# One new issue order, and a new deal of the PSUM banks, for a fused attention, mixture-of-experts and MLP kernel

## The chip, the cores and the metric

The kernel runs on one core of a Trainium2 chip. The metric is the device time of one execution in microseconds (us); the median of three executions of the kernel before is 450.44 us (449.55 to 452.05).

## The reference

Three blocks follow one another on float32 data. Each is written here with what matters for the work on the engines.

```python
# 1. block attention: 2 x 8 heads, 768 positions, head size 64
k_sum = max of k over blocks of 32;  v_sum = mean of v over blocks of 32     # 24 blocks
scores = [ q k^T / 8 where |i - j| < 16, else -1e9 ;  q k_sum^T / 8 + log 32 ]
a = softmax(scores);   x = a @ [v ; v_sum]                                    # [2, 768, 512]
# 2. mixture of 4 attention experts, the best 2 of them for each position
logits = x @ w_gate;  w = softmax over the top 2
out = sum over e of  w[e] * ( causal softmax(q_e k_e^T / 8) @ v_e ) @ wo[e]   # q_e = x @ wq[e], ...
# 3. mixer
u = out + (x^T U V)^T            # rank 32 along the positions
result = u + relu(u @ w_ch1) @ w_ch2                                          # 512 -> 2048 -> 512
```

## The kernel before

All of it is one program on one core, with five engines that each work through a queue of their own in order: TensorE (PE) does matrix products, VectorE (DVE), ScalarE (ACT) and GpSimd (POOL) the rest, and SyncE (SP) starts the DMAs.

**The work** is cut into some 830 parts. A part is a small function, mostly a generator that yields between its steps: one step puts the matmuls on PE, the next one the instruction that takes their result out of PSUM, and so on. The parts that the text speaks of:

- Preparation: `load_k`, `load_q`, `load_v` (DMAs), `fill_k` (L317 copies the mask columns), `ksum` and `vsum` (block maxima and means of the keys and values; L333 and L340 are matmuls on a tile 32 columns wide, L337 and L343 the copies behind them).
- Attention, 48 slots of two heads by 128 queries: `a_scores` (L385, four matmuls onto column tiles 64 wide; DVE minimum L388, ACT exponential L391), `a_trans` (L396, two transposes over the full width; ACT copy L398), `a_pv` (L408, four matmuls onto 64-wide tiles; DVE L415 to L417 after each second), `a_out` (L424, transposes over the full width; ACT L429, DVE L239).
- Experts: `v_proj` (L569, 12 matmuls, full width), `qk_proj` (L620, 12 matmuls, full width; ACT L625, DVE L239, and four POOL copies in `hi_pool`, L236), `s_row` (L651, full width; DVE L659, ACT L662), `s_norm` (DVE L669 and L670, POOL L675), `t_bank` (L684, transposes; ACT L692 or DVE L690), `pv` (L704, matmuls onto 64-wide tiles; ACT L711, DVE L713 or L708).
- Weights that are made while the experts run: `late_woT` and `wo_split` (DMA, ACT, then POOL L470 and L489), `w1_load` (DMA, L245) and `w1_split` (DVE L253, ACT L255, DVE L257, ACT L264, POOL L266). `w1_load` puts its data where `late_woT` had its own, so its DMA waits for L470.
- The mixer: `w1c` (L497), `mlp1` (L816; ACT L821, DVE L823), `mlp2` (L829), `resid` (L838), `store` (L849, L851, L853).

**The order** is a table. Each part has a number u, and `TIMES[u][i]` is the place of its step i among all 1891 steps. A heap hands the steps out by that place; what a step issues goes to the end of each engine's queue. So the table sets, engine by engine, what stands behind what; when an instruction runs depends on the semaphores that it waits for. The PSUM bank of a part's result comes from `BANKS[u]`:

```python
heapq.heappush(todo, (TIMES[u][0] if TIMES else t, u, 0, fn, args))               # in at()
return BANKS[part] if BANKS else i                                               # in bank_of()
t, u, i, fn, args = heapq.heappop(todo)                                          # the loop at the end
heapq.heappush(todo, (TIMES[u][i + 1] if TIMES else t + wait, u, i + 1, part, ()))
# a_scores: out rows 64u..64u+63 of the bank, 120 columns per head
pe.matmul(scb[64 * u:64 * u + 64, hh], QAT[..][hh][..], KWT[..][hh][:, 2 * t + u, :], start=True, stop=True)
# a_trans: full width
pe.transpose(tb[0:KCOL, 128 * u:128 * u + 128], ex[:, u, :], ident)
```

Of the kernel before, what the change touches and what calls it, by code (L numbers as in the profile page):

```python
# [35 lines left out]
def f(ap):  # L36
# [12 lines left out]
    (20,), (0,), (50,), (2, 3, 5), (26, 32, 40), (1,), (4,), (10,), (12, 17, 41), (13, 35), (23,), (15, 21), (18,),  # L49
    (162,), (25, 51), (8,), (29, 53), (11,), (6,), (354,), (57, 61, 66), (85, 91), (100,), (56, 59, 63), (88, 99),  # L50
    (115, 121), (154, 167, 174), (68, 75, 82), (94, 104), (127,), (65, 72, 76), (90, 108), (130, 137), (159, 207, 216),
    (77, 89, 96), (120, 129), (139,), (73, 78, 84), (116, 135), (147, 161), (183, 187, 196), (106, 114, 118),
    (152, 160), (166,), (97, 102, 111), (158, 164), (169, 177), (194, 198, 208), (103, 109, 138), (163, 172), (189,),
    (110, 117, 125), (150, 175), (191, 200), (222, 237, 255), (122, 128, 146), (184, 192), (210,), (126, 132, 153),
    (186, 195), (212, 230), (249, 260, 268), (176, 193, 211), (219, 224), (242,), (201, 213, 218), (228, 232),
    (243, 247), (258, 270, 323), (173, 188, 202), (221, 239), (282,), (197, 220, 229), (257, 264), (285, 291),
    (302, 312, 338), (214, 223, 241), (246, 250), (284,), (203, 236, 245), (261, 289), (293, 304), (313, 317, 326),
    (231, 238, 254), (287, 292), (306,), (251, 263, 273), (297, 301), (309, 311), (319, 344, 360), (244, 278, 283),
    (298, 305), (329,), (290, 300, 308), (315, 321), (335, 363), (373, 388, 393), (267, 272, 279), (303, 316), (357,),
    (271, 288, 294), (322, 339), (358, 371), (394, 412, 416), (310, 318, 324), (349, 366), (377,), (325, 332, 346),  # L60
    (367, 376), (380, 383), (395, 402, 406), (333, 343, 355), (372, 378), (413,), (342, 348, 362), (368, 385),
    (414, 420), (423, 434, 447), (345, 356, 369), (397, 405), (451,), (382, 387, 407), (426, 431), (453, 455),
    (501, 504, 508), (389, 404, 415), (436, 450), (473,), (361, 379, 390), (445, 464), (475, 479), (503, 507, 521),
    (411, 422, 460), (481, 483), (492,), (408, 425, 438), (478, 487), (493, 516), (524, 549, 580), (448, 452, 458),
    (484, 491), (498,), (364, 410, 435), (482, 494), (500, 510), (526, 534, 541), (465, 472, 476), (528, 537), (543,),
    (468, 489, 497), (512, 520), (544, 559), (584, 587, 596), (488, 515, 522), (527, 530), (575,), (533, 538, 542),
    (551, 562), (578, 588), (602, 606, 615), (495, 499, 509), (565, 568), (592,), (545, 550, 558), (566, 590),
    (597, 607), (621, 647, 653), (536, 564, 572), (579, 583), (598,), (548, 556, 560), (581, 595), (601, 611),
    (620, 625, 631), (540, 563, 570), (617, 623), (639,), (593, 603, 609), (614, 627), (640, 642), (656, 659, 681),
    (589, 600, 612), (616, 619), (672,), (586, 618, 629), (658, 665), (674, 678), (700, 704, 715),  # L70
    (9, 14, 16, 19, 22, 24, 27, 30, 31, 33, 37, 38, 44, 46, 49, 52, 54, 58, 62), (36, 45, 47, 48, 64, 87, 92, 98, 144),
    (28, 34, 43, 67, 74, 80, 83), (79, 86, 93, 107, 136, 148, 157), (7, 42), (55, 60, 69), (39, 70),
    (95, 105, 113, 119, 123, 131, 156), (134, 149, 165, 171, 209, 217, 226), (71, 143), (124, 133, 141), (81, 142),
    (151, 170, 179, 185, 190, 199, 206), (233, 259, 266, 276, 280, 286, 296), (112, 145), (101, 168, 181), (180, 205),
    (240, 248, 256, 262, 269, 277, 295), (275, 334, 340, 353, 359, 365, 375), (155, 182), (204, 215, 227), (234, 253),
    (281, 314, 320, 327, 331, 341, 347), (384, 391, 399, 401, 417, 463, 469), (225, 235), (252, 328, 336), (307, 352),
    (433, 437, 441, 444, 449, 457, 459), (400, 443, 454, 474, 505, 511, 514), (337, 351), (418, 421, 428), (370, 430),
    (461, 471, 480, 486, 490, 496, 502), (506, 519, 532, 535, 539, 546, 552), (398, 429), (392, 409, 470), (462, 485),
    (265, 381, 386), (274, 330, 374), (140, 178, 299), (350, 396, 403), (456, 466, 477), (427, 440, 442),
    (419, 424, 432), (439, 446, 467), (513, 518, 523), (517, 525, 529), (531, 547, 561, 567, 571, 573, 622, 626, 630),  # L80
    (553,), (569, 576, 585, 591, 594, 599, 604), (557, 574, 577, 582, 608, 610, 613), (554,), (555,), (624, 633, 637),
    (634, 638, 644), (650, 652, 675, 679), (684, 689), (695, 699), (688, 692), (723, 741, 745), (636, 661, 667),
    (654, 657, 671), (682, 685, 690, 694), (702, 707), (729, 734), (643, 669, 676), (641, 673, 680),
# [1020 lines left out]
```

## Time and profile before

| what | value |
|---|---|
| median of three executions | 450.44 us (449.55 to 452.05) |
| span of the profiled execution | 451.4 us |
| PE busy | 432.3 us, 96% of the span |
| DVE, ACT, POOL busy | 52%, 49%, 40% |
| chain that ended last | PE 94%, DMA 2%, the rest 1% or less each |

The profile gives the span of the profiled execution, from its first to its last instruction; it is 1.0 us above the median of the three timed ones. A busy share is the time in which an engine has an instruction under way; the matmuls are pipelined and overlap, so a busy PE may still lose time between two of them, and that shows only in the distance from one start to the next. The chain follows the work back from the last instruction, at each step to what released it.

### The profile page before, as it was taken

Reading aid. Unit: us, or ns where it says so; the run is one execution under the profiler, and the core shown is the slowest. Engines: PE = TensorE matmul, PEld = TensorE weight load, DVE = VectorE, ACT = ScalarE, POOL = GpSimd, SP = SyncE. Lnnn points to the kernel's source line nnn. Section 1 sums busy time; section 2 is a strip of 40 time slices with the busy share of each in tenths; the row PEclk is TensorE's granted clock in tenths of the full one; section 3 lists DMA queues with packets and bytes.
Section 4 is the critical chain, followed back from the end, with each engine's and each line's share of the span. In section 5 each row is a group of like instructions: output and inputs, shape, how many; then the busy total and the mean of one; then the engine's idle time right before and its main releaser. Section 6 shows DMA issues by size and latency. Waiting matters only on the chain.

```text
span 451.4 us, 8626 instructions
## 1 busy us (share of the span) xinstructions
PE 432.3 (96%) x3224; PEld 376.2 (83%) x3224; DVE 233.7 (52%) x633; ACT 219.1 (49%) x581; POOL 178.4 (40%) x252
## 2 busy tenths in 40 slices
PE   0799999999999999899999999999999999999996
PEld 0687889999889888678889899898888888888985
DVE  4488755767656778968877545343412111111112
ACT  4377865656667587887655544344321111111112
POOL 6784884337765698862235423322210000000000
PEclk9999999999999999999999999999999999999999
DMA  8897742000000032252336342222103000000003
GB/s 211 173 258 186 194 113 57 2 1 0 19 3 1 1 105 82 69 185 73 111 121 185 112 172 93 70 97 91 48 26 115 0 1 0 0 2 0 1 0 139
DMA packets 14473, 35.19 MB, mean 78 GB/s; under 512 B 1888, under 2 KB 3168, under 8 KB 14432
## 3 DMA queue, kind: packets, MB, share of 16 engines
q1 hardware_dynamic: 14432, 34.65, 25.5%
q8 instruction: 25, 0.41, 0.4%
q14 instruction: 16, 0.13, 0.1%
HBM read 31.50 MB, written 3.15 MB: 77 GB/s over the span
## 4 chain that ended last, share of the span: by engine, by line
PE 94%; DMA 2%; POOL 1%; DVE 1%; SPq 1%; issue 1%; ACT 0%; POOLq 0%
PE ps L829 29%; PE ps L816 15%; PE ps L620 8%; PE ps L385 5%; PE ps L704 5%; PE ps L497 5%; PE ps L651 4%; PE ps L684 4%; PE ps L569 4%; PE ps L838 4%; PE ps L408 3%; PE ps L396 3%; DMA vb<-in_vW_dram 2%; PE ps L333 2%; PE ps L424 1%; PE ps L340 1%
## 5 line engine op out<-in xcount | busy, mean ns | idle before, releaser
L823 DVE SCALAR_TENSOR_TENSOR a<-ps,a 128x384 fp32r<-128x384 f32 x64 | 35.0, 556 | 114.6 <-ACT a L821 114.6
L821 ACT ACTIVATE a<-ps 128x384 fp32r<-128x384 f32 x64 | 30.7, 491 | 114.1 <-PE ps L816 92.4
L816 PE MATMUL ps<-x,w1h 128*128 128x384 f32 x256 | 73.3, 338 | 0.0
L829 PE MATMUL ps<-m,a 128*128 128x512 f32 x216 | 52.6, 392 | 0.0
L816 PEld LDWEIGHTS ps<-x,w1h 128*128 128x128 f32 x256 | 47.1, 188 | 2.1 <-issue 0.4
L829 PEld LDWEIGHTS ps<-m,a 128*128 128x128 f32 x216 | 40.3, 188 | 7.8
L236 POOL TENSOR_SCALAR a<-a 64x384 fp32r<-64x384 f32 x64 | 33.7, 528 | 24.0 <-ACT a L625 18.4
L816 PE MATMUL ps<-x,w1l 128*128 128x384 f32 x128 | 43.2, 337 | 0.0
L620 PE MATMUL ps<-x,m 128*128 128x384 f32 x192 | 36.9, 342 | 0.0
L620 PEld LDWEIGHTS ps<-x,m 128*128 128x128 f32 x192 | 33.1, 188 | 0.5 <-DVE gmx L607 0.4
L675 POOL TENSOR_SCALAR ex<-ex,rs,gate 128x256 f32<-128x256 f32 (+5 forms) x36 | 25.9, 729 | 10.9 <-DVE rs L670 7.5
L651 PE MATMUL ps<-a 128*128 128x384 f32 (+4 forms) x128 | 27.9, 337 | 1.4 <-DVE nmx L659 1.4
L829 PE MATMUL ps<-vb,a 128*128 128x512 f32 x108 | 26.6, 392 | 0.0
L829 PE MATMUL ps<-v,a 128*128 128x512 f32 x108 | 26.1, 394 | 0.0
L257 DVE SCALAR_TENSOR_TENSOR x<-x 128x256 uint32<-128x256 uint32 (+3 forms) x38 | 24.7, 653 | 2.5 <-ACT x L255 2.4
L662 ACT ACTIVATE ex<-ex,nmx 128x256 f32<-128x256 f32 (+5 forms) x36 | 23.4, 652 | 4.8 <-DVE nmx L659 4.4
L816 PEld LDWEIGHTS ps<-x,w1l 128*128 128x128 f32 x128 | 24.0, 188 | 1.7
L388 DVE TENSOR_REDUCE nmx<-ps 128x2 f32<-128x240 f32 x48 | 19.1, 404 | 11.2 <-PE ps L385 10.2
L659 DVE CUSTOM_DVE_ANT_0 ex<-ps,cc 128x256 f32<-128x256 f32 (+5 forms) x36 | 21.1, 598 | 6.3 <-PE ps L651 4.1
L829 PEld LDWEIGHTS ps<-v,a 128*128 128x128 f32 x108 | 20.3, 188 | 4.4
L829 PEld LDWEIGHTS ps<-vb,a 128*128 128x128 f32 x108 | 20.0, 188 | 3.6
L651 PEld LDWEIGHTS ps<-a 128*128 128x128 f32 x128 | 19.9, 189 | 3.7 <-DVE nmx L659 2.2
(218 smaller groups left out, 923.3 us busy)
## 6 DMA issues: line engine op xcount, KB each, us to landing
x<-in_w_dram SPq DMA_DIRECT2D x16, 512.0 KB, 3.6
x<-in_w_dram SPq DMA_DIRECT2D x20, 256.0 KB, 2.9
vb<-in_vW_dram SPq DMA_DIRECT2D x5, 585.0 KB, 4.9
a<-in_kP_dram SPq DMA_DIRECT2D x7, 416.0 KB, 5.2
out_dram<-a SPq DMA_DIRECT2D x10, 256.0 KB, 2.1
x<-in_wm_dram SPq DMA_DIRECT2D x4, 386.0 KB, 5.3
tb<-in_w_dram SPq DMA_DIRECT2D x6, 256.0 KB, 3.0
a<-in_w_dram SPq DMA_DIRECT2D x6, 256.0 KB, 2.8
```

Source lines behind the costliest of these rows:

```text
L236: pool.tensor_scalar(dst, src, 1.0, 0.0, op0=ALU.mult, op1=ALU.add)
L257: dve.scalar_tensor_tensor(low, high, 3, low, op0=ALU.logical_shift_left, op1=ALU.bitwise_or)
L385: pe.matmul(scb[64 * u:64 * u + 64, hh], QAT[p % NK][hh][:, QT * (2 * t + u):QT * (2 * t + u) + QT], KWT[p % 2][hh][:, 2 * t + u, :], star ...
L497: pe.matmul(acc, wo[k][:, int(a == 2), 128 * c:128 * c + 128], w[k][:, int(a == 1)], start=j == 0, stop=j == 11)
L620: pe.matmul(acc, (WML if wl else WMH)[k][:, 128 * e:128 * e + 128], xt(b, k, xl)[:, c], start=n == 0, stop=n == 11)
L651: pe.matmul(flat[:, base + c0:base + c1], QS[u][:, 128 * i:128 * i + 128], kk[:, c0:c1], start=x == 0, stop=x == 1)
L662: act.activation(ex[:, 0:W], ex[:, 0:W], AF.Exp, bias=nmx, scale=-1.0, accum_out=sums)
L675: pool.tensor_scalar(ex, ex, rs[:, i % 2:i % 2 + 1], gate[b][:, i, e:e + 1], op0=ALU.mult, op1=ALU.mult)
L816: pe.matmul(acc, (W1L if wl else W1H)[ff // 2][:, c, 128 * (ff % 2):128 * (ff % 2) + 128], cp(b, c, xl)[:, o], start=n == 0, stop=n == 5)
L821: act.activation(h, acc, AF.Relu)
L823: dve.scalar_tensor_tensor(l, acc, 0.0, f(h), op0=ALU.max, op1=ALU.subtract)
L829: pe.matmul(out_bank(b, 3 * j + t), a[:, 128 * t:128 * t + 128], w, start=False, stop=ff == 15 and x == 2, skip_group_check=True)
```

## The change

The two tables get other numbers; no other line changes. The kernel after has the same 1891 steps and the same 4103 instructions, in another order on each queue, and another bank for many results. The new tables take three lines more, so that L385 of before is L388 after, and so on for all that follows.

```diff
 TIMES = [
-    (20,), (0,), (50,), (2, 3, 5), (26, 32, 40), (1,), (4,), (10,), (12, 17, 41), (13, 35), (23,), (15, 21), (18,),
...
 BANKS = [
...
-    3, -1, -1,
+    -1, 3, -1, 1, -1, -1,
 ]
```

What the tables do to the queues is seen in the instructions themselves. First PE in the attention, some 20 us into the program. A row is a line of the code, the operation, what is written and read, the shape of the output and how many follow one another. `pt`, `c`, `w1h`, `w1l`, `ex`, `tb` and `vb` are buffers in SBUF, `cc` holds constants, `ps` is PSUM. 64x120 is a step of `a_scores`, 64x65 one of `a_pv` (four matmuls a step), 120x128 `a_trans` and 128x128 `a_out`. Before:

```order
L424 MATMUL ps<-cc,pt_82 128x128 x2
L396 MATMUL ps<-cc,tb 120x128 x4
L408 MATMUL ps<-vb,pt_79 64x65 x4
L408 MATMUL ps<-vb,w1h_88 64x65 x4
L424 MATMUL ps<-cc,pt_82 128x128 x2
L385 MATMUL ps<-pt_80,w1h_88 64x120 x2
L385 MATMUL ps<-c_81,w1h_88 64x120 x2
```

After, at the same point of the work:

```order
L411 MATMUL ps<-vb,pt_79 64x65 x4
L388 MATMUL ps<-pt_80,w1h_88 64x120 x2
L388 MATMUL ps<-c_81,w1h_88 64x120 x2
L411 MATMUL ps<-vb,w1h_88 64x65 x8
L411 MATMUL ps<-vb,pt_79 64x65 x4
L388 MATMUL ps<-pt_80,w1h_88 64x120 x2
L388 MATMUL ps<-c_81,w1h_88 64x120 x2
L388 MATMUL ps<-w1h_85,ex 64x120 x2
L388 MATMUL ps<-w1l_86,ex 64x120 x2
L399 MATMUL ps<-cc,ast 120x128 x2
```

The 64-wide steps, two or three at a time between full-width ones before, now stand seven in a row here (and two more `a_scores` steps right ahead of these rows). Over the whole program PE goes from full width to 64 wide 33 times before and 17 times after, and from 64 wide to full width 36 times before and 18 after. The 43 runs of 64-wide steps (28 in the attention, 15 of `pv`) become 24 (17 and 7). The switches to and from the 32-wide tiles of `vsum` and `a_mat` are 31 in both.

Second, DVE at the start, ahead of the first scores. `a_90` holds the mask columns, `ks` the block maxima, `pt_80` and `c_81` the keys of the first head pair. Before:

```order
L317 COPY pt_80<-a_90 64x1200
L368 TENSOR_SCALAR c_81<-ks 64x2x24
L337 COPY vt<-ps 128x128
L343 COPY vs<-ps 24x128
L874 MEMSET w1l_87 32x24
L317 COPY c_81<-a_90 64x1200
L388 TENSOR_REDUCE nmx<-ps 128x2 x5
```

After:

```order
L320 COPY c_81<-a_90 64x1200
L357 TENSOR_REDUCE ks<-a_89 128x24
L371 TENSOR_SCALAR c_81<-ks 64x2x24
L340 COPY vt<-ps 128x128
L371 TENSOR_SCALAR pt_80<-ks 64x2x24
L371 TENSOR_SCALAR c_81<-ks 64x2x24
L320 COPY w1h_85<-a_90 64x1200
L391 TENSOR_REDUCE nmx<-ps 128x2 x2
```

The mask copy into `c_81` stood behind the two copies of `vsum` and stands ahead of them now. On PE, the second matmul of that `vsum` (L340 before, L343 after) moves from ahead of all scores to behind two steps of them.

Third, POOL in the experts' stretch, some 165 us into the program. `v` is the split weight of `late_woT`, `a` the queries and keys of an expert, `ex` and `vb` rows of probabilities, `x` staging. Before:

```order
L470 TENSOR_TENSOR v_2112<-x_2119,v_2112 128x256
L236 TENSOR_SCALAR Usb<-x_2119 128x192
L470 TENSOR_TENSOR v_2110<-x_2119,v_2110 128x256
L675 TENSOR_SCALAR vb<-vb,rs_2272,gate_74 128x768
L236 TENSOR_SCALAR a_1266<-a_1266 64x384 x2
L675 TENSOR_SCALAR vb<-vb,rs_2272,gate_74 128x640
L675 TENSOR_SCALAR ex<-ex,rs_2357,gate_74 128x256
L675 TENSOR_SCALAR vb<-vb,rs_2357,gate_74 128x128
L489 TENSOR_TENSOR wol<-x_2119,woh 128x512
L470 TENSOR_TENSOR v_2109<-x_2119,v_2109 128x256
L470 TENSOR_TENSOR v_2111<-x_2119,v_2111 128x256
```

After:

```order
L678 TENSOR_SCALAR ex<-ex,rs_2281,gate_74 128x384
L239 TENSOR_SCALAR a_1068<-a_1068 64x384
L473 TENSOR_TENSOR v_1397<-x_1404,v_1397 128x256
L239 TENSOR_SCALAR a_1068<-a_1068 64x384
L473 TENSOR_TENSOR v_1394<-x_1404,v_1394 128x256
L473 TENSOR_TENSOR v_1396<-x_1404,v_1396 128x256
L473 TENSOR_TENSOR v_1395<-x_1404,v_1395 128x256
L678 TENSOR_SCALAR vb<-vb,rs_2293,gate_74 128x768
L239 TENSOR_SCALAR a_1068<-a_1068 64x384 x3
L678 TENSOR_SCALAR vb<-vb,rs_2293,gate_74 128x640
```

The four subtractions of `late_woT` stood in two pairs, eight instructions apart. They now stand almost together, ahead of one probability row and of the last three `hi_pool` copies of an expert's queries and keys.

## Rows read from the trace of the kernel before

**Rows 1.** The page: busy us, share of the span and instructions of each engine.
```profile
PE 432.3 (96%) x3224; PEld 376.2 (83%) x3224; DVE 233.7 (52%) x633; ACT 219.1 (49%) x581; POOL 178.4 (40%) x252
```
**Rows 2.** Busy time by stretch: us; PE, PEld, DVE, ACT, POOL; clock; DMA share; GB/s.
```profile
180.00:200.00 20.00, 18.38 (x132) 13.85 (x131) 15.72 (x49) 16.17 (x45) 16.15 (x23) 1.00 0.43 145
220.00:440.00 220.00, 220.00 (x1114) 194.51 (x1113) 78.25 (x155) 68.09 (x153) 37.44 (x38) 1.00 0.18 60
```
**Rows 3.** Timeline of PE, attention: start, us, line, tile, contraction*output rows, moving shape, matmuls.
```profile
23.58 0.45 PE L408 MATMUL ps<-vb,w1h 120*64 120x65 f32 x8
23.82 0.43 PE L385 MATMUL ps<-w1h,pt 128*64 128x120 f32 x4
...
31.88 0.42 PE L385 MATMUL ps<-c,w1h 128*64 128x120 f32 x4
32.24 0.44 PE L424 MATMUL ps<-cc,pt 128*128 128x128 f32 x2
32.51 0.60 PE L396 MATMUL ps<-cc,tb 128*120 128x128 f32 x4
33.04 0.46 PE L408 MATMUL ps<-vb,pt 120*64 120x65 f32 x8
33.33 0.45 PE L408 MATMUL ps<-vb,w1h 120*64 120x65 f32 x8
33.71 0.44 PE L424 MATMUL ps<-cc,pt 128*128 128x128 f32 x2
```
**Rows 4.** Chain of waits: start, us, engine and line, matmuls.
```profile
24.04 1.23 PE ps L385 x24
...
30.27 0.22 PE ps L396 x2
...
34.15 1.38 PE ps L385 x24
...
102.69 2.11 PE ps L620 x12
...
105.47 2.31 PE ps L620 x12
```
**Rows 5.** Timeline of PE at the start, with the idle time ahead and its releaser.
```profile
12.80 1.51 PE L333 MATMUL ps<-vb,cc 96*32 96x128 f32 x24 [12.80 <-DMA vb<-in_vW_dram]
14.72 0.62 PE L340 MATMUL ps<-vt,cc 128*24 128x128 f32 x2 [0.40 <-DVE vt L337]
15.77 0.67 PE L385 MATMUL ps<-pt,ex 128*64 128x120 f32 x4 [0.43 <-issue]
16.61 0.67 PE L385 MATMUL ps<-c,ex 128*64 128x120 f32 x4 [0.17 <-issue]
...
17.43 0.65 PE L385 MATMUL ps<-c,ex 128*64 128x120 f32 x4
```
**Rows 6.** Timeline of DVE at the start.
```profile
15.73 0.78 DVE L317 COPY c<-a 64x1200 f32<-64x1200 f32 x1
```
**Rows 7.** Timeline of PE in the experts.
```profile
186.67 0.85 PE L651 MATMUL ps<-a 128*128 128x320 f32 x4 [1.37 <-DVE nmx L659]
```
**Rows 8.** Timeline of DVE in the experts.
```profile
172.62 1.49 DVE L253 TENSOR_SCALAR x<-x 128x256 uint32<-128x256 uint32 x1 [0.68 <-POOL ex L675]
...
187.39 0.29 DVE L253 TENSOR_SCALAR x<-x 128x256 uint32<-128x256 uint32 x1
...
195.53 0.30 DVE L253 TENSOR_SCALAR x<-x 128x256 uint32<-128x256 uint32 x1 [2.14 <-DMA x<-in_w_dram]
```
**Rows 9.** Timeline of POOL in the experts.
```profile
172.65 1.30 POOL L489 TENSOR_TENSOR wol<-x,woh 128x512 fp32r<-128x512 f32 x1
...
187.35 0.89 POOL L675 TENSOR_SCALAR ex<-ex,rs,gate 128x512 f32<-128x512 f32 x1 [0.42 <-DVE rs L670]
```
**Rows 10.** Groups by line on POOL: busy us, mean ns, idle time before.
```profile
L470 POOL TENSOR_TENSOR v<-x,v 128x256 fp32r<-128x256 f32 x4 | 3.0, 748 | 0.0
```
**Rows 11.** DMA issues on the page: count, KB each, us from issue to landing.
```profile
x<-in_w_dram SPq DMA_DIRECT2D x20, 256.0 KB, 2.9
```

266 rows, old and new, of tables (BANKS, TIMES) are left out of this document.

## The prediction

> **What bounds the kernel now.** I read the page first, for the share of each engine [rows 1]: PE has an instruction under way in 432.3 of 451.4 us, and no other engine passes 52%. Then the chain of waits, of which the table above gives the shares: PE 94%. Then the busy time by stretches, to see whether the rest is spread out [rows 2]. It is not. From 20 us to the end of the mixer PE is busy throughout (220.00 of 220.00 from 220 to 440); the one stretch of 20 us that is not full is 180 to 200, where 1.62 us are idle, and most of that is a single wait of 1.37 us for the DVE minimum L659 [rows 7]. The rest of the idle time lies at the start: PE waits 12.80 us for the first half of the values [rows 5], and after its last matmul the end has a copy and a DMA. So PE's own work sets the end, and a change that only reorders can pay in three ways: fewer microseconds for the same matmuls, an earlier start, or less waiting.
>
> A busy PE is still not one that loses nothing. Its matmuls overlap, so the next view is the timeline of PE, read by the distance from one start to the next [rows 3], with the chain beside it [rows 4].
>
> **The change part by part.**
>
> *Switches of the tile width.* A step of `a_scores` (8 matmuls of the trace) takes 0.41 us when its own kind stands around it: 24 in 1.23 us [rows 4]; half a step is 0.205. A step of `a_pv` takes 0.24 (23.58 to 23.82) [rows 3], two transposes 0.22 [rows 4]. Now the same steps where the width changes [rows 3]:
> - Leaving 64 wide for the full width: the last half step of scores takes 0.36 instead of 0.205 (31.88 to 32.24), the last `a_pv` step 0.38 instead of 0.24 (33.33 to 33.71). That is 0.14 to 0.155 more. The first transposes after it take 0.27 instead of 0.22 (32.24 to 32.51), 0.05 more. Together 0.20 a switch.
> - Leaving the full width for 64 wide: four transposes take 0.53 instead of 0.44 (32.51 to 33.04), 0.09 more, and the first `a_pv` step after them 0.29 instead of 0.24 (33.04 to 33.33), 0.05 more. Together 0.14.
>
> The chain gives the same by another road [rows 4]: the first 24 score matmuls after full-width work take 1.38 instead of 1.23, 0.15 more, and 12 matmuls of `qk_proj` behind 64-wide work take 2.31 instead of 2.11, 0.20 more. Going from one half of the array to the other costs nothing: both column tiles are used within the 0.41.
>
> The order has 36 switches from 64 wide to the full width before and 18 after, and 33 the other way before and 17 after: 18 x 0.20 = 3.6, and 16 x 0.14 = 2.2, so 5.8 us less. If every switch were the 0.15 that the chain shows for one direction, 34 of them are 5.1; if every one were 0.20, 6.8. All of it lies on the path, since PE is what everything waits for in the stretches where these steps stand. The 32-wide tiles have 31 switches in both, and I cost them at nothing.
>
> *The start.* The same bytes lie ahead of the first `vsum`, so I leave PE's first matmul at 12.80. Its 24 matmuls end at 14.31 [rows 5]. Before, the scores begin at 15.77, do half a step, and stand until 16.61, because the mask copy into `c` runs only from 15.73 to 16.51 [rows 5, 6]. After, that copy stands ahead of both copies of `vsum` on DVE, and is done while PE is still in `vsum`. The scores run at half speed here: a step takes 0.82 (16.61 to 17.43) [rows 5] instead of 0.41, the lower of the clock's two levels by the spacing. Before, they are thus as far as if they had begun at 16.61 - 0.41 = 16.20 and never stopped. If they begin at 14.31 after, that is 1.9 us earlier, but the second matmul of `vsum`, which filled the hole before, now stands among the scores and costs its 0.62 [rows 5]: a gain of 1.3 at best. At worst the scores still begin where they do now, because of the queries that are loaded behind the values, and lose the 0.62. Between +0.6 and -1.3 I take -0.5, a little on the good side of the middle, since what ended the hole at 16.61 is gone for sure.
>
> *Waits in the experts.* Before, PE loses 1.6 us between 180 and 200 [rows 2]. The new order changes what queues where. Four POOL subtractions L470 of 0.75 us each, 3.0 in all [rows 10], stood in two pairs and now stand nearly together, ahead of three `hi_pool` copies that the scores of the seventh expert wait for. Behind them comes SP: the first DMAs of `w1_load` write where L470 reads, so they start later, and a DMA of that kind lands 2.9 us after its issue [rows 11]. Behind the DMA comes DVE: two L253 that wait for it stand ahead of an L659, of a copy of transposes and of an addition L713 on DVE's queue. Such a block can be survived: at 195.53 DVE stood 2.14 us for the DMA of an L253 [rows 8], in a stretch in which PE lost 1.6 us in all, with 1.37 of it elsewhere [rows 2, 7]. The bounds: no wait at all is 1.6 us less than now; one DMA in full and two of the subtractions are 2.9 + 1.5 = 4.4 more. I take +0.5, near the one block that the trace shows, which cost almost nothing.
>
> *A rule that speaks against it.* An L253 took 0.29 us at 187.39 and 1.49 at 172.62 [rows 8]; the slow one ran beside POOL's L489, from 172.65 to 173.95, the quick one beside POOL's L675, from 187.35 on [rows 9]. So DVE stood still for a POOL instruction with two tensor inputs, and not for one with a single one; L470 is of the first kind. The Trainium skill (SBUF — State Buffer, "SBUF: two separate sides") says that DVE and GpSimd share a port pair as an exclusive lock, the loser blocking for the other's whole instruction. The slow L253 agrees with that; the quick one, beside L675, does not. By the page each of three L253 in this stretch would wait for a POOL instruction of some 0.9 us, 2.7 of DVE's time; if half of it reached PE the sum would be about 1.3 higher.
>
> *The rest.* The mixer's order changes too, but it has no 64-wide tile, and PE is full in it [rows 2]; I cost it at nothing, with PE's own backlog as the cover. The end has the same copy and DMA. The new banks add no instruction; where one makes a matmul wait for an earlier reader, that is in the bounds of the waits.
>
> *The sum.* -5.8 - 0.5 + 0.5 = -5.8. The profiled span of 451.4 becomes 445.6; it lies 1.0 above the median of the timed runs, so the time is 444.6 us, 1.3% less.
>
> **The rivals.**
> 1. *The saving stays and the waits eat most of it.* One block of DVE in full and two subtractions, 4.4 us more than now instead of 0.5: 444.6 + 3.9 = 448.5. For it: POOL, ACT and DVE are each busy for 15.7 to 16.2 of 20 us from 180 to 200 [rows 2], so a late one catches up slowly. Against it: PE lost 1.6 us there under the old order, with a block of 2.14 in it.
> 2. *Slower: the queue of DVE behind two late weight loads sets the pace.* Both L253 wait out their DMA one after the other, 5.8 us, behind all four subtractions, 3.0, and the second meets a POOL instruction, 1.2 more (1.49 less 0.29 [rows 8]): 10.0 instead of 0.5 gives 444.6 + 9.5 = 454.1. It decides once the waits pass some 8 us more than forecast. Against it: the two DMAs overlap, and the minimum behind them has some slack.
> 3. *The waits go as well.* The stall of 1.37 us behind L659 [rows 7] belongs to one meeting of instructions that the new order breaks up, and the start gains its full 1.3: 451.4 - 5.8 - 1.3 - 1.6 = 442.7, less 1.0 is 441.7.
> 4. *The switches are not what costs.* If the extra time at a switch were waiting for operands that happens to fall there, it would be lost elsewhere: 450 to 451. Against it: the same 0.14 to 0.20 appear with four kinds of steps, and the steps that have their own kind around them never show them.
>
> **How the numbers follow.** The forecast has 0.60, rival 1 0.17, rival 2 0.06, rival 3 0.13, rival 4 0.04. The forecast's own range is 442.5 to 447, from the bounds of the switches (-6.8 to -5.1) and of the start. I reach to rival 3 below and past rival 1 above: 441.0 to 449.5, which leaves out rivals 2 and 4 and some edge. A change of under 0.5% (2.25 us) can hardly be told from none here. Below 448.2 lie the forecast, rival 3 and a third of rival 1: 0.79. Within 0.5% lie the rest of rival 1 and rival 4: 0.15. Above 452.7 lies rival 2: 0.06.
>
> **What would show it.** Right: in the chain, pieces of L385 and L408 (three lines later in the new numbering) that are longer and fewer, with the normal 0.41 and 0.24 a step inside; PE's summed busy time near 426; the scores without a hole before 16.6 us. Wrong: a stretch between 140 and 200 us in which PE is not full by 3 us or more, with a wait for DVE's L659 or POOL's L236 as its end, or an L253 on DVE with an idle time of some 3 us for a DMA ahead of it; or PE busy still near 432 with 34 fewer switches, which would be rival 4.

## The result, and the profile after

The changed kernel takes 455.19 us (median of 4 runs, 455.06 to 457.26), the kernel before 450.9 in the same runs (449.55 to 452.05): a ratio of 1.0112, 95% interval 1.0081 to 1.0144. It is slower by 4.3 us where 5.8 less were forecast. The time is outside the range, and it lies near rival 2's 454.1, but not by rival 2's mechanism.

All line numbers of the changed kernel are three higher. The page after, the busy time of each engine and the chain's shares by engine:

```profile
PE 429.8 (95%) x3224; PEld 377.3 (83%) x3224; DVE 229.0 (51%) x633; ACT 217.4 (48%) x581; POOL 179.3 (40%) x252
...
PE 82%; DMA 5%; DVE 5%; POOL 2%; ACT 2%; issue 2%; SPq 1%; POOLq 0%; DVEq 0%
```

PE has 2.5 us less under way than before [rows 1], in a span that is 2.0 longer (453.4). The prediction's signs were a busy time near 426 if it is right and near 432 for rival 4; 429.8 is neither, since a part of the waits counts as busy. The chain tells more: PE's share fell from 94% to 82%, and the DMAs and DVE stand in it now. Where that is, the busy time by stretches shows (us; PE, PEld, DVE, ACT, POOL; clock; DMA share; GB/s):

```profile
40.00:60.00 20.00, 17.01 (x314) 14.18 (x312) 13.66 (x44) 14.15 (x44) 13.49 (x15) 1.00 0.90 228
...
160.00:180.00 20.00, 18.95 (x136) 16.04 (x137) 13.38 (x43) 14.76 (x41) 16.90 (x26) 1.00 0.28 90
180.00:200.00 20.00, 18.38 (x145) 14.81 (x144) 17.00 (x50) 16.90 (x46) 15.34 (x20) 1.00 0.38 135
200.00:220.00 20.00, 18.68 (x137) 14.43 (x136) 14.24 (x33) 15.20 (x35) 6.86 (x7) 1.00 0.19 65
220.00:440.00 220.00, 220.00 (x1113) 194.44 (x1113) 74.67 (x154) 67.09 (x153) 36.09 (x37) 1.00 0.18 58
```

Four stretches of 20 us have holes where one had [rows 2]: 3.0 us in the attention, 1.0, 1.6 and 1.3 in the experts. The MLP is as it was. Holes understate waits, because a matmul is drawn as busy to its modelled end. So I also took, for every step of PE after 20 us, the distance from its first matmul to the next step's, less the usual distance of such a step in the trace of before, switches of the width included. What is left over, the waits by distance, sums to 1.2 us before (2.9 from 160 to 220 us, and -1.8 in small pieces elsewhere) and to 10.4 after (3.7 from 40 to 60 us, 6.7 from 160 to 220).

**The switches.** The rows that answer to [rows 3]; PE's timeline after, in the attention:

```profile
30.96 0.42 PE L388 MATMUL ps<-pt,w1h 128*64 128x120 f32 x4
31.17 0.42 PE L388 MATMUL ps<-c,w1h 128*64 128x120 f32 x4
31.52 0.65 PE L399 MATMUL ps<-cc,tb 128*120 128x128 f32 x4
32.05 0.44 PE L427 MATMUL ps<-cc,pt 128*128 128x128 f32 x2
32.42 0.43 PE L388 MATMUL ps<-pt,w1h 128*64 128x120 f32 x4
32.68 0.38 PE L388 MATMUL ps<-c,w1h 128*64 128x120 f32 x4
```

A half step of scores takes 0.21 (30.96 to 31.17) and 0.35 ahead of a switch (31.17 to 31.52); the first one behind a switch 0.26. Where the earlier trace had 0.36 and 0.205 [rows 3, 4], this one has 0.35 and 0.21: a switch costs what it did, and there are 34 fewer.

**The start.** PE's timeline after:

```profile
10.84 1.51 PE L336 MATMUL ps<-vb,cc 96*32 96x128 f32 x24 [10.84 <-DMA cc<-in_vB_dram]
13.80 0.67 PE L388 MATMUL ps<-pt,ex 128*64 128x120 f32 x4 [1.46 <-DVE pt L371]
...
15.75 0.62 PE L343 MATMUL ps<-vt,cc 128*24 128x128 f32 x2
...
19.16 0.61 PE L388 MATMUL ps<-c,ex 128*64 128x120 f32 x4
19.70 0.53 PE L399 MATMUL ps<-cc,tb 128*120 128x128 f32 x2
```

The hole of [rows 5] inside the scores is gone, as forecast, but a hole of 1.46 us ahead of them is new, for the DVE step L371 that fills the last columns of the scaled keys. The same 74 matmuls (24 of `vsum`, 2 of its second half, 48 of scores) end at 19.70 - 10.84 = 8.86 us behind the first one. Before they took 8.03, from 12.80 to the second of the next two rows, which are of the trace before:

```profile
20.51 0.39 PE L385 MATMUL ps<-c,ex 128*64 128x120 f32 x4
20.83 0.43 PE L333 MATMUL ps<-vb,cc 96*32 96x128 f32 x8
```

The two are not quite alike. Half steps stand 0.40 us apart at the start and 0.205 later; that halving came at 20.4 us before, 7.6 behind the first matmul, and at 20.0 after, 9.1 behind it. The second trace of before (before_again, below), where it also came 9.1 behind, took 8.41 for the same matmuls. Against that one the new start is 0.5 us longer and not 0.8.

**The attention.** The three longest waits of PE there:

```profile
43.35 0.87 PE L336 MATMUL ps<-vb,cc 96*32 96x128 f32 x24 [0.63 <-DMA vb<-in_vW_dram]
...
48.59 0.43 PE L388 MATMUL ps<-c,pt 128*64 128x120 f32 x4 [1.93 <-DMA pt<-in_qT_dram]
...
53.61 0.43 PE L388 MATMUL ps<-w1l,w1h 128*64 128x120 f32 x4 [0.37 <-DMA w1h<-in_qT_dram]
```

All three are loads. The longest load in the chain after, and the stretch of 40 to 60 us before:

```profile
43.37 10.10 DMA w1h<-in_qT_dram
```

```profile
40.00:60.00 20.00, 20.00 (x338) 16.09 (x338) 14.83 (x48) 16.21 (x53) 16.40 (x18) 1.00 0.69 194
```

SP's queue shows why they are late; its timeline before, and then after (issue, us, line, what is loaded):

```profile
29.07 0.33 SPq L325 DMA_DIRECT2D vb<-in_vW_dram  x1
29.44 2.36 SPq L303 DMA_DIRECT2D pt<-in_qT_dram  x2
```

```profile
34.74 0.33 SPq L301 DMA_DIRECT2D a<-in_kP_dram  x1
35.12 0.47 SPq L306 DMA_DIRECT2D pt<-in_qT_dram  x1
35.68 0.53 SPq L328 DMA_DIRECT2D vb<-in_vW_dram  x1
36.31 0.47 SPq L306 DMA_DIRECT2D w1h<-in_qT_dram  x1
36.83 2.10 SPq L518 DMA_DIRECT2D x<-in_wm_dram  x2
38.98 0.47 SPq L306 DMA_DIRECT2D pt<-in_qT_dram  x1
```

Before, both query loads of `load_q(4)` left from 29.44 on, ahead of the next key load. After, the key load `load_k(5)` stands first and waits at the head of SP's queue until 34.74 for its buffer, which POOL (L377) and DVE (L357) still read. The queries leave at 35.12 and, behind two loads of expert weights, at 38.98. In 40 to 60 us the DMA engines are 0.90 busy (0.69 before), and the chain has a query load of 192 KB issued at 43.37 that takes 10.10 us to land, where such loads took 5.2 to 5.5 in the median before.

**The experts.** PE, then DVE after (what answers to [rows 7, 8]):

```profile
172.78 1.04 PE L654 MATMUL ps<-a 128*128 128x384 f32 x5 [0.58 <-POOL a L239]
...
186.41 0.66 PE L687 MATMUL ps<-cc,ex 128*128 128x128 f32 x4 [1.62 <-POOL ex L678]
...
202.26 0.55 PE L687 MATMUL ps<-cc,ex 128*128 128x128 f32 x3 [0.87 <-POOL ex L678]
```

```profile
166.76 0.42 DVE L716 TENSOR_TENSOR c<-ps,tb 64x256 f32<-64x256 f32 x1 [2.57 <-ACT tb L714]
...
192.28 0.30 DVE L256 TENSOR_SCALAR x<-x 128x256 uint32<-128x256 uint32 x1 [1.87 <-DMA x<-in_w_dram]
```

The row on POOL and the row on ACT that stand behind two of these waits:

```profile
185.44 0.92 POOL L678 TENSOR_SCALAR ex<-ex,rs,gate 128x640 f32<-128x640 f32 x1
```

```profile
165.75 0.71 ACT L471 CAST v<-x 128x256 fp32r<-128x256 f32 x2 [2.48 <-PE ps L707]
```

The stall of [rows 7] behind the minimum is gone. POOL ends the waits now. The first, of 0.58, is the meeting that the prediction had in view: the `hi_pool` copies L239 run behind the four subtractions. The longest, of 1.62, is another: the normalisation L678 that feeds the transposes runs at 185.44, behind five copies and subtractions of other steps. The DVE wait of 2.57 comes from ACT, where a copy of weights L471 stood 2.48 us for the matmuls L707 that still read what it overwrites. One L256 waited 1.87 us for its DMA, like the one of 2.14 before [rows 8].

### The profile page after: what moved, and what is told of

It is laid out like the page before. It is cut to its first block, busy times and chain, and to the rows that moved or that the text cites. A ratio compares the mean times of both kernels' runs of the same rounds, so it can differ in the third digit from the quotient of the medians.

```text
span 453.4 us, 8600 instructions
## 1 busy us (share of the span) xinstructions
PE 429.8 (95%) x3224; PEld 377.3 (83%) x3224; DVE 229.0 (51%) x633; ACT 217.4 (48%) x581; POOL 179.3 (40%) x252
## 4 chain that ended last, share of the span: by engine, by line
PE 82%; DMA 5%; DVE 5%; POOL 2%; ACT 2%; issue 2%; SPq 1%; POOLq 0%; DVEq 0%
PE ps L832 29%; PE ps L819 15%; PE ps L623 6%; PE ps L388 5%; PE ps L500 4%; PE ps L841 4%; PE ps L572 4%; PE ps L654 3%; PE ps L707 3%; PE ps L411 2%; PE ps L399 2%; DMA w1h<-in_qT_dram 2%; PE ps L687 2%; DMA x<-in_w_dram 2%; DMA cc<-in_vB_dram 1%
## 5 line engine op out<-in xcount | busy, mean ns | idle before, releaser
L819 PE MATMUL ps<-x,w1h 128*128 128x384 f32 x256 | 74.5, 338 | 0.0
L239 POOL TENSOR_SCALAR a<-a 64x384 fp32r<-64x384 f32 x64 | 34.3, 535 | 21.3 <-ACT a L628 14.3
L678 POOL TENSOR_SCALAR ex<-ex,rs,gate 128x256 f32<-128x256 f32 (+5 forms) x36 | 26.2, 735 | 9.7 <-DVE rs L673 6.0
L662 DVE CUSTOM_DVE_ANT_0 ex<-ps,cc 128x512 f32<-128x512 f32 (+5 forms) x36 | 20.9, 595 | 4.5 <-PE ps L654 2.8
L256 DVE TENSOR_SCALAR x<-x 128x256 uint32<-128x256 uint32 (+3 forms) x38 | 16.1, 435 | 13.1 <-DMA x<-in_w_dram 11.5
```

The costliest lines, as they stand in the source:

```text
L239: pool.tensor_scalar(dst, src, 1.0, 0.0, op0=ALU.mult, op1=ALU.add)
L662: dve.tensor_tensor_reduce(out=ex[:, 0:W], in0=flat[:, base:base + W], in1=cmask[:, S - W:S], scale=-1.0 / 8.0, scalar=3.0e38, op0=ALU.add ...
L678: pool.tensor_scalar(ex, ex, rs[:, i % 2:i % 2 + 1], gate[b][:, i, e:e + 1], op0=ALU.mult, op1=ALU.mult)
L819: pe.matmul(acc, (W1L if wl else W1H)[ff // 2][:, c, 128 * (ff % 2):128 * (ff % 2) + 128], cp(b, c, xl)[:, o], start=n == 0, stop=n == 5)
```

## The experiments

Each run's ratio is to the kernel before on the same chip. "Waits" are the sums by distance described above.

**The attention's loads: e1_queries.** The changed kernel with three query loads moved:

```diff
 L328 DMA vb<-in_vW_dram
+L306 DMA pt_79<-in_qT_dram x2
 L301 DMA a_89<-in_kP_dram
-L306 DMA pt_79<-in_qT_dram
 ...
-L306 DMA pt_79<-in_qT_dram
```

> The order after, with three query loads moved forward on SP: both of the fifth head pair ahead of the sixth pair's keys, and the second of the sixth pair ahead of three weight loads of 386 KB; nothing else moves. In the trace of after PE loses 3.7 us more than its steps take between 40 and 60 us, 2.2 of it for one query load that landed 9.5 us after its issue, 0.6 for another, 1.0 for a load of values. Theory A (the place in SP's queue is the cause): the two query waits go, 2.8 us or more, about 452.3 against 455.2. Rival B (the DMA engines are simply full in this stretch, so that another transfer comes late in their place): within 1 us of 455.2.

Measured: 452.63 us (10 runs), ratio 1.0047 [1.0019, 1.0074], 2.6 below the change, as theory A had it. The waits from 40 to 60 us fell from 3.7 to 2.0; the two for queries are gone, and a transpose L399 now waits 0.88 us for its exponential. The late queries are a cause, worth 2.6 us.

**The weights of the experts: e2_weights, e3_both, e4_w2only.** The steps that load and split weights are put back among PE's steps where they stood before; all of them, all and the queries, and the queries with `w2_load` and `w2_split` alone. The first, on SP:

```diff
-L468 DMA x_1404<-in_woT_dram
-L488 DMA x_1404<-in_wo_dram x2
-L468 DMA x_1404<-in_woT_dram x3
+L488 DMA x_1404<-in_wo_dram
+L468 DMA x_1404<-in_woT_dram x2
+L488 DMA x_1404<-in_wo_dram
+L468 DMA x_1404<-in_woT_dram x2
```

> The order after, in which only the steps that load and split weights (late_woT, wo_split, w1_load, w1_split, w2_load, w2_split) stand where the order before had them against PE's work; in the order after they stand up to 136 steps earlier. Between 160 and 220 us PE loses 6.7 us in waits after, 2.9 before. Theory A (weights pulled forward overfill DVE, ACT and POOL while the experts need them): the 3.8 us go, 451.4 against 455.2. Rival C (the new order of the experts' own steps makes the waits): no change beyond 1 us, 454.2 to 456.2.

> Both edits together: the three query loads forward and the weight steps back. Theory A: the gains add, 2.8 + 3.8 = 6.6, about 448.6, below the kernel before. Rivals B and C: 454 to 456. If the saving of the tile switches (5.8) were not real, the waits gone would bring it to before's 450.9 and not below.

> The queries forward as in the first run, and of the weights only the second MLP matrix's loads and splits (w2_load, w2_split) back at their old place; late_woT and the splits of the first matrix stay pulled forward. If the w2 splits, which fill DVE to 9.84 of 10 us between 180 and 190, carry the loss in the experts: within 1 us of the run with both edits, about 449. If the early late_woT and w1 steps carry it (POOL's four subtractions together, DVE behind two late loads): about 452.

Measured: 459.25 (ratio 1.0192 [1.0138, 1.0246]), 456.93 (1.0136 [1.0092, 1.0179]) and 452.36 (1.0036 [1.0016, 1.0056]). None of the theories for the first two held: weights at their old places make it worse by 4 us. The matmuls L500 that use them stand earlier in the new order and then wait for the split (1.1 us for L267 alone). Behind that hole both traces also show the granted clock at its lower level, 0.50, from 190.8 to 194.2 us in e2_weights (PE was busy for 0.94 of the 2 us from 188 to 190); at half rate that is up to 1.7 us of the 4, by estimate. So the early weights are not shown to be a cause of the loss. `w2` makes no difference (0.3 us).

**The kernel before once more: before_again.** No edit.

> The kernel before once more, for a second trace of it. Its executions spread from 449.1 to 453.1 us; the trace that the prediction was read from has a span of 451.4, and a time is 1.8 above its span in all runs, so it was one of the longest. Theory: its length came from the start, where PE waited until 12.80 us for the values; here the first matmul starts near 11 and the span is 448 to 449.5, with the same waits later. Rival: the start is the same and the spread is in the experts' stretch (180 to 200 us).

One run of 452.85 us, span 451.0, first matmul at 12.74. The theory missed both numbers for this run (first matmul near 11, span 448 to 449.5), because the first load landed late again. With the profiles of the two price tests below (whose attention and experts are unchanged) it explains the span; see the last point of the next section.

**The same saving by other moves: e5_merged and e8_small.** The kernel before, with its own banks, and neighbours exchanged so that narrow steps stand together: in e5_merged 100 switches become 66, with steps up to 39 places away (its expectation says 28); in e8_small 78, none by more than 7 places. From e8_small, steps on PE:

```diff
 a_trans(13)
+vsum(3).0
 a_scores(18)
-vsum(3).0
 ...
 a_scores(20)
+a_scores(19)
 a_trans(16)
 a_out(11)
-a_scores(19)
 a_trans(15)
```

> The order and banks before, with 21 local moves of one to four PE steps past a neighbouring run of steps, so that PE changes tile width 66 times instead of 100, as often as in the order after; no step stands more than 28 of 1891 places from its old one, and the DMAs stay where they are. By the distances of starts in the trace of before, the switches that go are worth 5.8 us. Theory (a switch costs 0.14 to 0.20 us and the loss after is waits alone): 450.6 - 5 = 445.5, 444.5 to 447. Rival 4 of the prediction (the time at a switch is a wait that would fall elsewhere): 450 to 451.

> The kernel before with its own BANKS, and only those neighbours in its order exchanged that save a switch of the tile width at a distance of at most 7 places (14 exchanges: switches 100 -> 78, where the change and the earlier merged order go to 66; 92 of the 1891 steps stand elsewhere, none by more than 7 places). Theory A (each switch costs its 0.14 to 0.20 us everywhere, and what ate the saving so far were the long displacements, by which a step comes before its data or a load behind another load's wait): TensorE's work falls by 22 x 0.17 = 3.7 us, waits grow by under 1.5 us, time 448 to 449 (ratio about 0.994). Rival B (whatever groups the narrow steps makes waits as large as the switches it saves, however short the distance, since the narrow steps are the ones that hand work to the other engines and their results are then wanted closer together): work falls by the same 3.7 but waits grow by 3.5 or more, time 450.5 or more (ratio 0.999 or above).

Measured: 461.2 (ratio 1.0204 [1.0163, 1.0245]) and 454.75 (1.0092 [1.0071, 1.0114]). Both have fewer switches, and both lose more to waits by distance: 12 us more than before in e5_merged, 6.4 in e8_small. The trace of e5_merged is of its quickest execution, 457.89 us at a mean granted clock of 0.999; the other five, 459.60 to 462.44, show 0.991 to 0.996, so part of the median is the clock. PE's timeline of e8_small:

```profile
36.10 0.87 PE L335 MATMUL ps<-vb,cc 96*32 96x128 f32 x24 [0.37 <-ACT ex L393]
...
39.75 0.43 PE L398 MATMUL ps<-cc,ex 128*120 128x128 f32 x2 [0.30 <-ACT w1h L400]
...
43.25 0.46 PE L410 MATMUL ps<-w1l,pt 120*64 120x65 f32 x8 [0.43 <-DVE vs L345]
```

Before, no such wait stood between 20 and 60 us. The first two are at the very places of the diff: `vsum(3)` pulled ahead of a score step meets a bank that an exponential still reads, and a transpose pulled closer to its forerunner meets ACT's copy. They are short, and by distance there are nine of over 0.25 us from 35 to 80 us. In e5_merged neither theory nor rival came near 461.2. In e8_small rival B held in time: moves of a few places undo the saving. But both runs keep banks that were dealt for the old order, and the first of these waits is for a bank. No run here has these orders with a new deal of the banks, nor the change's order with the banks of before, so the two parts of the change, order and banks, are not told apart.

**Moves in the experts: e6_moves.** e1_queries with nine steps moved between 160 and 190 us; for one, the weight copies behind the copies of `pv` on ACT:

```diff
 L665 ACTIVATE vb,sums
+L714 COPY tb<-ps x2
 L471 CAST v<-x
 L471 CAST v<-x
-L714 COPY tb<-ps x2
```

> The order after with the query loads forward (the first run), and in the experts three things moved: POOL's second normalisation of the seventh expert's last rows directly behind the first instead of six POOL instructions later; late_woT's four ACT copies behind the ACT copies of pv, which they held up by 2.5 us while PE still read the values they overwrite; two of its four POOL subtractions and the two DVE steps that wait for the next weights behind the work of the scores. In the trace of the first run PE loses 6.0 us from 160 to 220, of it 1.45 at the first of these, 0.86 + 0.49 + 0.32 + 0.21 at the others. Theory A' (queue places of single instructions make the waits): 2 to 3 us less than 452.6, about 450. Rival (DVE and POOL are simply overfull there, and a wait removed comes back at the next step): 452 or more.

Measured: 453.76, ratio 1.0068 [1.0041, 1.0096]. The waits aimed at shrank (1.45 to 0.3 us), and a new one of 2.6 us by distance came at a scores step in the same stretch:

```profile
174.45 0.90 PE L654 MATMUL ps<-a 128*128 128x320 f32 x2 [1.99 <-ACT pt L695]
```

Here too the granted clock falls: it is 0.50 from 174.5 to 177.9 us, after PE was busy for 0.46 of the 2 us from 172 to 174. The time is the rival's (452 or more), and the ratio lies within the interval of e1_queries.

**The price of a switch by itself: p1_apart to p4_f32_together.** The MLP, where PE never waits. Two of the six matmuls of each of 64 tiles become 64 columns wide, apart (two round trips of the width) or together (one); in the first pair in the MLP's own type, in the second in float32 as the narrow matmuls of the attention are:

```diff
-pe.matmul(acc, (W1L if wl else W1H)[...], cp(b, c, xl)[:, o], ...)
+p = slice(0, 64 if n in (1, 3) else 128)       # together: (2, 3)
+g = f if n in (1, 3) else lambda ap: ap        # second pair only
+pe.matmul(acc[p], g((W1L if wl else W1H)[...][:, p]), g(cp(b, c, xl)[:, o]), ...)
```

> The kernel before, with the second and the fourth of the six matmuls of each MLP tile (64 tiles, line 816, in 220 to 440 us, where TensorE never waits) made 64 columns of the tile wide instead of 128, a wide one between them: no instruction more, two round trips of the tile width per tile. It leaves out the other half of these two products. Theory A (a change of width to 64 and back costs 0.20 + 0.14 us, as read from the distances of steps): 128 round trips x 0.34 = 43.5 us more, time about 494. Rival B (the switches are not what the time goes into; the distances at switches are long for another reason, the narrow matmuls' own first and last columns or the cold load of weights): the narrow matmuls take as long as wide ones and the time stays within 2 us, 449 to 453.

> As the run before it, but the third and the fourth of the six matmuls are the narrow ones, side by side: the same instructions, one round trip of the width per tile. It leaves out the other half of these two products. Theory A: 64 x 0.34 = 21.8 us more than before, about 472.5, and 21.8 less than with the two apart. Rival B (a narrow matmul itself costs more, whatever stands beside it): the same time as with the two apart, both above before. Rival C (no price at all): within 2 us of before.

> As the run with the narrow matmuls apart (second and fourth of the six of each MLP tile 64 columns wide), but these two also in plain float32, as every narrow matmul of the attention and the experts is, where those of the first two tests kept the faster type of the MLP. It leaves out the other half of these two products. By itself it says little, since float32 makes the two matmuls longer; it is to be held against the next run, which has the same instructions in another place. Theory A (a round trip to float32 matmuls of 64 columns costs 0.09 + 0.10 to 0.20 us, as the distances in the attention and the experts show: 0.20 from a transpose to a narrow matmul where two transposes stand 0.11 apart): 64 round trips x 0.2 to 0.34 = 13 to 22 us above the next run. Rival B (the price does not come from the width at all): within 2 us of the next run.

> The same instructions as in the run before it, with the two narrow float32 matmuls of each tile side by side (third and fourth of six): one round trip of the width per tile in place of two. It leaves out the other half of these two products. Theory A: 13 to 22 us below the run before it. Rival B: within 2 us of it.

Measured: 450.67 and 450.56 in the first pair (ratios 1.0015 [0.9995, 1.0036] and 1.0002 [0.9984, 1.0021]): no price at all, as rivals B and C had it. In float32 554.23 and 533.03: 21.2 us for 64 round trips, 0.331 us each, with the same instructions in another order, at the upper end of theory A. One tile of each; apart, then together:

```profile
303.06 0.33 PE L818 MATMUL ps<-x,w1h 128*128 128x384 f32 x1
...
305.55 0.34 PE L818 MATMUL ps<-x,w1h 128*128 128x384 f32 x1
```

```profile
302.76 0.34 PE L818 MATMUL ps<-x,w1h 128*128 128x384 f32 x1
...
304.92 0.34 PE L818 MATMUL ps<-x,w1h 128*128 128x384 f32 x1
```

From the first to the sixth matmul it is 2.49 us apart and 2.16 together. The price is real and is that of the prediction (0.34), but for float32 matmuls and not for the width as such. In these two runs the type changes wherever the width does, so by themselves they do not tell a price of both together from one of the type alone. The trace of before has a change of width between float32 matmuls: the half step of scores ahead of `vsum`, 64 to 32 wide, takes 0.32 us (20.51 to 20.83) instead of 0.205, against 0.36 ahead of the full width [rows 3]; so part of the price comes without a change of type. A full-width float32 product among the narrow ones, which would settle it, was not run.

**Restoring the distances: o4_after, o3_before, o5_after, o7_after.** In o4_after and o3_before steps of all engines are moved by a search that keeps each consumer as far behind its producer, and the queue ahead of it, as the durations in the traces ask (887 and 700 steps elsewhere; 69 and 88 switches). o5_after takes only the experts of o4_after, with the attention of e1_queries and the start and MLP of the change; o7_after all of o4_after but its start and MLP:

```diff
 o5_after, steps of all engines:
 up to 62 us: as e1_queries
-62 us to 218 us: as the change
+62 us to 218 us: as o4_after
 from 218 us: as the change
```

> The changed kernel's BANKS, with an order in which the narrow steps stay grouped (69 switches; 66 in the changed kernel, 100 before) and the steps of all engines are placed so that no step of TensorE stands closer behind the step that feeds it than that step and the queue ahead of it take by the durations of the traces, loads included (887 steps stand elsewhere, none by more than 47 places). Theory A (the switches saved are worth their 31 x 0.17 = 5 us, and what ate them in the changed kernel and the three earlier orders was that consumers and loads were placed too close): waits after 20 us fall from 10 to 3 us or less, time 443 to 447, faster than both kernels. Rival B (waits come back in another place whatever is moved, as in the run with the nine moves, since the other engines are nearly full in the experts): time 450 or more.

> The same done to the kernel before, with its own BANKS: 88 switches in place of 100, 700 steps elsewhere, none by more than 36 places. Theory A: 12 x 0.17 = 2 us of work less and the 2.4 us of waits between 180 and 200 us gone: 445.5 to 448. If spacing alone counts and the switches are worth nothing: 448, and the run with 69 switches is not below it by more than 1 us. Rival B: 450 or more.

> The order of the run o4_after, kept only between the attention's 60 us and the MLP; up to there the order of e1_queries (the changed kernel with its query loads issued early), and from the MLP on the changed kernel's own (66 switches). Measured from the first matmul, the trace of o4_after lay 1.7 us below that of before although TensorE waited 2.4 us between 41 and 46 us and ran 46 to 48 us at half the clock; and its first matmul came at 13.4 us in place of 10.8 to 12.8, its last store 1.1 us later after the last matmul. Theory A (distances matter, place by place): waits of e1_queries up to 60 us (2.5 us), those of o4_after from 160 to 220 us (3.3), together 5.8 in place of the changed kernel's 10.4 us, so 455.2 - 4.6 = 450.6, and with the first matmul as in most runs 449 to 451.5, within 0.5% of before. Rival B (the waits in the experts follow from what the attention leaves behind, so they come back when the attention is exchanged): 452.5 or more.

> The order of o4_after with only its first 17 us and its part from the MLP on put back to the changed kernel's (70 switches). Theory A: the wait at 41 to 46 us and the half clock behind it stay (a reduction on VectorE still waits for a load there while three large weight loads share the DMA engines), but the first matmul comes at about 11 us again and the last store 1.1 us earlier: 13.4 + 432.5 + 5.2 becomes 10.9 + 432.5 + 4.2 = 447.6 us of span, 449.4 us of time, 1.5 us below before. Rival B (the first matmul's time is scatter, not order, and the first 17 us of the changed kernel cost waits of their own): 451.5 or more.

Measured: 452.64 (ratio 1.0034 [1.0013, 1.0054]), 452.57 (1.0042 [1.0029, 1.0055]), 449.72 (0.9974 [0.9957, 0.9990]) and 451.45 (1.0012 [0.9992, 1.0032]). The first two came out with rival B (450 or more), the third with theory A, and the fourth at rival B's edge (451.5). In o4_after a hole in the attention cost twice. PE's timeline, then two stretches:

```profile
44.38 1.37 PE L336 MATMUL ps<-vb,cc 96*32 96x128 f32 x24 [1.18 <-ACT ex L394]
```

```profile
42.00:44.00 2.00, 0.96 (x10) 0.53 (x10) 1.64 (x7) 1.97 (x6) 1.06 (x2) 1.00 1.07 234
44.00:46.00 2.00, 1.62 (x26) 1.26 (x27) 0.57 (x3) 0.38 (x2) 1.84 (x3) 0.65 0.98 272
46.00:48.00 2.00, 2.00 (x10) 1.68 (x8) 1.47 (x6) 1.12 (x3) 1.82 (x4) 0.50 1.07 300
```

PE was idle for half of 42 to 44 us, and the granted clock fell to 0.50, the lower of its two levels. o5_after, without that hole, is faster than both kernels, by 1.1 us against before and 5.5 against the change:

```profile
40.00:60.00 20.00, 19.01 (x326) 16.07 (x320) 14.75 (x51) 15.68 (x50) 17.12 (x19) 1.00 0.75 197
...
180.00:200.00 20.00, 18.56 (x152) 15.65 (x154) 16.19 (x47) 17.05 (x44) 15.76 (x20) 1.00 0.24 82
200.00:220.00 20.00, 20.00 (x125) 16.81 (x125) 14.88 (x31) 14.60 (x34) 4.13 (x5) 1.00 0.23 79
```

Its holes in these stretches are 2.4 us against the change's 5.9. It differs from e1_queries only between 62 and 218 us, and is 2.9 us quicker (3.2 when each is held against its own kernel before). So the waits in the experts, like the late queries, come from the order, and another order of the same steps takes a part of them away. The saving comes back only in part: 5.1 us of waits remain by distance. Whether some order has all of it is open.

From the first matmul's start to the last one's, the traces show 434.1 to 434.5 us before, 438.4 in the change, 432.5 in o4_after, 433.0 in o7_after and 432.0 in o5_after, but 434.4 in o3_before: there the search gained nothing between them, and the end behind the last matmul is 1.0 us longer, as in o4_after (5.2 against 4.1 to 4.2). Distances kept by the search were thus not enough by themselves.

## Why the prediction was wrong, point by point

- **The switches, -5.8: right.** 34 fewer are 17 round trips; at the 0.331 us measured by themselves that is 5.6. The float32 pair speaks against rival 4: there PE never waits, and the price shows in the whole time. The reason I gave was too wide: the same change of width was free in the MLP's type.
- **The start, -0.5 (bounds +0.6 to -1.3): no gain.** It measured 8.86 - 8.03 = +0.8 in the two traces, of which 0.4 is the moment at which the half rate ended; against before_again it is +0.5. I took away one hole and did not ask what the scores would meet when they came earlier: the last columns of the keys, 1.46 us.
- **The waits, +0.5 (bounds -1.6 to +4.4): the step that failed.** They measured +9.2 (10.4 less 1.2). Two things were missed. The attention had no term at all: PE was full there, so I read a stretch without holes as one with room, though the moved steps included SP's loads and the DMA engines were about 0.7 to 0.8 busy; the late queries are worth 2.6 us (e1_queries). And in the experts I priced the one block that I saw coming, the four subtractions and the DMA behind them. They did stand together and ended one wait of PE, 0.58 us; the larger ones came from other meetings: L678 on POOL behind five instructions, an ACT copy behind matmuls that still read its target. Moving steps took 2.6 us (attention) and 2.9 (experts) away; the causes of the rest are read from the rows alone. My upper bound was a list of known blocks, and not a bound.
- **Rival 2** gave nearly the right time for another reason, which is luck: PE's longest waits name POOL and query loads, and one L256 waited for its DMA, by less than the L253 of [rows 8].
- **The rule of the Trainium skill** (SBUF — State Buffer, "SBUF: two separate sides") would have had three L253 wait for a POOL instruction each, 2.7 us of DVE's time. The 14 of them from 140 to 210 us have a median of 0.34 us and a longest of 0.79 (0.32 and 1.49 before). That price does not show in them.
- **The conversion, "1.0 above the median": right in size, by a wrong idea.** A run's time is its span plus 1.8 us (453.4 and 455.18 here, 449.0 and 450.81 in p2_together), so the traced run of before took some 453.2, an estimate. It was long mostly by its start. From the first matmul to the last it has 434.5 us, the three other traces with that attention 434.1 to 434.2, but its first load landed late, 12.80 us against, in p2_together,

```profile
10.80 1.51 PE L333 MATMUL ps<-vb,cc 96*32 96x128 f32 x24 [10.80 <-DMA vb<-in_vW_dram]
```

With the measured terms and the median of before, 450.9 - 5.6 + 9.2 + 0.5 = 455.0, against 455.19 measured. That it closes is no proof of the terms one by one: the waits are what the distances leave over once steps and switches have their usual price.

## What to carry to other kernels

A tuned order is a set of distances: where PE has no hole, the distances may be just long enough, and grouping like steps shortens some of them. Before crediting an order with a saving, follow every moved load and copy on its own queue, in the full stretches too, and look for the wait that the next engine has no slack for. Compare spans from the first matmul, and price a resource by the same instructions in two orders.

## What the runs showed that I had not expected

- Changing the tile width between 128 and 64 columns cost 0.331 us a round trip where the narrow matmuls were float32 and 0.00 (0.1 us over 64) in the MLP's faster type, with 384 columns moving in both. Why is open.
- The scores run at half their later rate at the start. The column of the granted clock reads 1.00 there, but for want of an entry: the trace's records of the clock begin at 20.4 us before, 20.0 in the change and 17.0 in o5_after, and in before and o5_after the half steps go from 0.40 to 0.205 us apart at just these points. So the spacing fits my reading, the lower of the clock's two levels, though no record states it. In o4_after the record does state it, 0.50 from 46 to 48 us, after PE was busy for 0.96 of the 2 us from 42 to 44.
- A load of 192 KB took 10.10 us to land in a stretch in which the DMA engines were 0.90 busy.
